# A retention and two mixture-of-experts layers on one core: the retention's state products in quarters of the array

## The chip, the cores and the metric

The kernel runs on one core of a Trainium2 chip. The metric is the device time of one execution in microseconds; of the kernel before, three runs are known, with a median of 594.36 us (592.88 to 595.75).

## What is computed

A retention (linear attention with a decay per head) over 4 batches, 8 heads, 768 tokens and 64 features feeds a soft mixture of experts, and that a top-2 mixture of experts. Only the first is touched by the change:

```python
gamma = 1.0 - 2.0 ** (-5.0 - np.arange(H, dtype=np.float32))
scale = 1.0 / np.sqrt(D)
state = np.zeros((B, H, D, D), dtype=np.float32)
for t in range(S):
    state = gamma[None, :, None, None] * state + np.einsum('bhd,bhe->bhde', k[:, :, t], v[:, :, t])
    y[:, :, t] = scale * np.einsum('bhd,bhde->bhe', q[:, :, t], state)
...
x = np.ascontiguousarray(attn_out.transpose(0, 2, 1, 3)).reshape(B * S, H * D)
x = _moe_ref(x=x, **moe_kwargs)
return _moe2_ref(x=x, **moe2_kwargs)
```

All of it is float32. The soft mixture needs the whole of x before its experts can start, so the retention (about the first 157 us) runs ahead of all else on TensorE; meanwhile SyncE's queue brings in q, k, v and the first expert weights (16 MB), and writes zeros to the output.

## The kernel before

The tokens are taken in 24 chunks of 128 (6 per batch, c = j % 6 is the place in the batch). A chunk's loop body (line 438) puts these steps on TensorE in this order; `put` ties each step behind the one before, so TensorE's order is the order of the text:

- `k_t(j+2)` (L281): four 128x128 transposes of K, copied out of PSUM by ScalarE (`kT`, L283).
- `inter(j)` (L310): the old state times Q, four products of 128x128 by 128x128. Two heads share a product: the state tile `sbd` is block-diagonal, so half of each is zeros. Not in the first chunk of a batch.
- `q_t` (L269): four transposes of Q, scaled out of PSUM by VectorE (`qT`, L274).
- `x_n(j-1)` (L343): four transposes of the last chunk's output `xT`, copied out by ScalarE (`x`, L345).
- `group1` (L381, `pd`), in every fourth chunk (j % 4 == 2).
- `qk(j+1)` (L292): eight products over 64 features, masked out of PSUM by VectorE into two `am` tiles (L296).
- `group0` (L354, `pl`) in chunks with j % 4 == 0 and `group2` (L391, `pp`) in those with j % 4 == 2: the soft mixture's logits, a running softmax on ScalarE and VectorE (`LT`, `al`, `dT`), and its weighted sum.
- `kv(j)` (L332): the new state, eight products into `pS`, copied by ScalarE into the two diagonal blocks of the other `sbd` tile (L337, two copies of 64x256). Not in the last chunk of a batch.
- `y_out(j)` (L320): eight products of V with `am`, added to the `py` bank that inter began; VectorE scales it into `xT` (L323).

After that, `spread(j+3)` (L253, L254) rearranges K of a later chunk on ScalarE (two copies of 64x512, into `comp` or `kl`) and V on GpSimd. Where ScalarE does this within its own order is the scheduler's choice. Three uses of PSUM share one tag, `pt`, with two buffers: k_t, q_t and x_n take it in turn, so x_n writes where k_t wrote and waits until ScalarE has copied kT away. `py` has two buffers of one bank, `pa` two, `pS` and `pg` one each: all eight banks are taken.

The loads of W1 (L479) are paced: each waits for a one-element VectorE copy of a chunk's `xT` (L478). K's and V's loads (L237) wait until ScalarE and GpSimd have emptied the buffer they go to.

Of the kernel before, what the change touches and what calls it, by code (L numbers as in the profile page):

```python
# [9 lines left out]
F32 = mybir.dt.float32  # L10
# [32 lines left out]
F1, F2, F3, F4 = 2, 0, 0, 26  # L43
FA, FT = 6, 3
RL = 1
XB = 6
FS, FU, FV = 10, 2, 2
TZ = 0, 4
BIG = 8192.0
# [5 lines left out]
def _const_table():  # L55
    j = np.arange(P)
    tok = 2 * (j % 64) + j // 64
    gam = 1.0 - 2.0 ** (-5.0 - np.arange(H, dtype=np.float64))
    cols = {}
    cols["mask"] = (tok[:, None] <= tok[None, :]).astype(np.float64)  # L60
    i = np.arange(64)
    gq = gam[None, :, None] ** (2 * i[None, None, :] + (j // 64)[:, None, None]) / np.sqrt(D)
# [42 lines left out]
def kernel(ctx: ExitStack, tc: tile.TileContext, q, k, v, phi, w1, w2,  # L105
# [103 lines left out]
    with ExitStack() as actx:  # L209
# [31 lines left out]
        def spread(j):  # L241
# [8 lines left out]
            gs = slice(64 * g, 64 * g + 64)  # L250
            for r in range(2):
                rs = slice(64 * r, 64 * r + 64)
                nc.scalar.copy(KL[j][rs], RAW[u][0][gs, :, r, :])  # L253
                pool_ins[0] = nc.gpsimd.tensor_tensor(VL[j][rs], RAW[u][1][gs, :, r, :],  # L254
                                        gv[gs, r, t, :, None].to_broadcast([64, H, D]), op=OP.mult)

        QT, KT, AM = {}, {}, {}
        sbd = []
        for i in range(2):
            s_t = io.tile([P, HP, P], F32, name=f"sbd{i}", bufs=1)  # L260
            nc.vector.memset(s_t, 0.0)
            sbd.append(s_t)

        def q_t(t, s):
            if s == 0:
                QT[t] = io.tile([P, HP, 2, P], F32, name="qT", bufs=2)
            pt = psA.tile([P, HP, P], F32, name="pt", tag="pt")
            for hp in range(HP):
                mm = nc.tensor.transpose(pt[:, hp, :], QL[t][:, 2 * hp + s, :, :], ident)  # L269
            o = QT[t].rearrange("p h g (r i) -> p h g r i", r=2)  # L270
            i = pt.rearrange("p h (g i) -> p h g i", g=2)
            for r in range(2):
                rs = slice(64 * r, 64 * r + 64)
                nc.vector.tensor_tensor(o[64 * s:64 * s + 64, :, :, r, :], i[rs],  # L274
                                        gq[rs, :, s, None, :].to_broadcast([64, HP, 2, 64]), op=OP.mult)
            return mm

        def k_t(j):
            pt = psA.tile([P, HP, P], F32, name="pt", tag="pt")
            for hp in range(HP):  # L280
                mm = nc.tensor.transpose(pt[:, hp, :], KL[j][:, 2 * hp:2 * hp + 2, :], ident)  # L281
# [4 lines left out]
        def qk(j):  # L286
            t, g = divmod(j, 2)
            pa = [psA.tile([P, HP, P], F32, name="pa", tag="pa") for _ in range(2)]
            for hp in range(HP):
                for s in range(2):  # L290
                    r = slice(64 * s, 64 * s + 64)
                    mm = nc.tensor.matmul(pa[s][:, hp, :], KT[j][r, hp, :], QT[t][r, hp, g, :],  # L292
                                          start=True, stop=True)
            for s in range(2):
                a = io.tile([P, HP, P], F32, name="am", bufs=3)
                nc.vector.tensor_tensor(a, pa[s], mask_b, op=OP.mult)  # L296
                AM[j, s] = a
            return mm

        pS = psA.tile([P, HP, D], F32, name="pS", bufs=1)  # L300
# [4 lines left out]
        def inter(j):  # L305
            t, g = divmod(j, 2)
            c = j % NC
            PY[j] = psA.tile([P, HP, P], F32, name="py")
            for hp in range(HP if c else 0):
                mm = nc.tensor.matmul(PY[j][:, hp, :], sbd[c % 2][:, hp, :], QT[t][:, hp, g, :],  # L310
                                      start=(hp == 0), stop=False, skip_group_check=True)
            return mm if c else None

        def y_out(j):
            c = j % NC
            py = PY.pop(j)
            am = [AM.pop((j, s)) for s in range(2)]
            for hp in range(HP):
                for s in range(2):
                    mm = nc.tensor.matmul(py[64 * s:64 * s + 64, hp, :], VL[j][:, 2 * hp + s, :],  # L320
                                          am[s][:, hp, :], start=(not c and hp == 0), stop=True, skip_group_check=True)
            XT[j] = work.tile([P, HP, P], F32, name="xT", bufs=4)
            nc.vector.tensor_tensor(XT[j], py, gy[:, c, :, None].to_broadcast([P, HP, P]), op=OP.mult)  # L323
            return mm

        def kv(j):
            c = j % NC
            if c == NC - 1:
                return
            for hp in range(HP):  # L330
                for s in range(2):
                    mm = nc.tensor.matmul(pS[64 * s:64 * s + 64, hp, :], KL[j][:, 2 * hp + s, :],  # L332
                                     VL[j][:, 2 * hp + s, :], start=(c == 0 and hp == 0),
                                     stop=True, skip_group_check=True)
            for s in range(2):
                r = slice(64 * s, 64 * s + 64)
# [81 lines left out]
        fill(psA, "py", FS)  # L418
        load_q(0)
        nc.sync.dma_start(cta, csta)  # L420
        load_kv(0)
# [3 lines left out]
        spread(0)  # L425
        for s in range(2):
            put(q_t, 0, s)
        fill(psA, "py", FU)
        put(k_t, 0)
        fill(psA, "py", FV)  # L430
        load_q(2)
        spread(1)
        load_kv(2)
# [4 lines left out]
        for j in range(NCH + 1):  # L438
            t, g = divmod(j, 2)
            if j < NCH:  # L440

                if j + 2 < NCH:
                    put(k_t, j + 2)
                put(inter, j)
                tn, s = (t + 1, 1) if g == 0 else (t + 2, 0)
                if tn < NT:
                    put(q_t, tn, s)
# [55 lines left out]
        pm = psA.tile([P, 4], F32, name="pm", tag="py")  # L503
        nc.tensor.matmul(pm, psel, m4, start=True, stop=True)
        group1(mg)
        fill(psA, "pa", 3)
# [7 lines left out]
        pz = psA.tile([P, 1], F32, name="pz", tag="py")  # L514
# [11 lines left out]
        for kd in range(KD):  # L526
# [4 lines left out]
        ph = psA.tile([P, QF], F32, name="ph", tag="py")  # L531
# [570 lines left out]
```

## Time and profile before

| what | value |
|---|---|
| median of 3 runs | 594.36 us (592.88 to 595.75) |
| profiled execution | span 596.2 us (the page gives no other time of it) |
| TensorE busy | 551.9 us (93%) |
| VectorE, ScalarE, GpSimd busy | 43%, 41%, 38% |
| mean granted clock of TensorE | 0.96 of full speed |
| DMA, whole span | 111.76 MB, mean 187 GB/s |
| the 20 `inter` steps | 160 instructions, 22.5 us busy |
| the 24 `qk` steps | 384 instructions, 29.0 us busy |

A float32 product appears as two TensorE instructions with two weight loads, so a step of four products counts x8. Busy time is the union of the instructions' spans, and overlapping instructions count once. How long a step holds TensorE is therefore read from the start of its first instruction to the start of the next step's. An engine can be busy nearly all the time and still start a step only because another engine has just finished.

### The profile page before, as it was taken

The numbers are of one execution on the slowest core, as the hardware profiler recorded it, in microseconds if no ns is written. First come the engines' busy times: TensorE is split into PE (matmuls) and PEld (weight loads), VectorE is DVE, ScalarE is ACT, GpSimd is POOL, SyncE is SP. The second block draws the span as 40 slices with busy tenths as digits, with TensorE's granted clock in tenths as the row PEclk, the third lists the DMA queues.
The fourth block names the chain that finished last, engine by engine and source line by source line (L and its number), as shares of the span: only waits on it lengthen the run. The fifth ranks groups of instructions, "written<-read, shape, count | busy, mean of one in ns | idle before, by whom it ended". The sixth has DMA issues, their size and how long they took to land. (4 is left out here: it accounts for less than half of the span.)

```text
span 596.2 us, 10652 instructions
## 1 busy us (share of the span) xinstructions
PE 551.9 (93%) x4176; PEld 418.9 (70%) x4176; DVE 254.6 (43%) x521; ACT 242.4 (41%) x529; POOL 224.0 (38%) x214
## 2 busy tenths in 40 slices
PE   6899999699899888799999999999999999999990
PEld 3787878578553345677787787787787787787870
DVE  3467777375303177834425225235235234324200
ACT  3565746344202235325426246256345345334200
POOL 3434634141103055445344434435344345432331
PEclk9799999799899898989999999999999999999996
DMA  9999999996699962446567566566656653644232
GB/s 251 246 273 308 236 323 379 349 349 236 257 384 410 379 211 68 96 96 167 131 138 186 109 146 181 109 149 181 128 141 174 133 122 55 138 101 51 38 40 33
DMA packets 79453, 111.76 MB, mean 187 GB/s; under 512 B 10034, under 2 KB 51570, under 8 KB 78498
## 3 DMA queue, kind: packets, MB, share of 16 engines
q1 hardware_dynamic: 65488, 94.75, 49.3%
q0 software_dynamic: 9696, 14.37, 17.4%
q10 hardware_dynamic: 4210, 1.87, 1.1%
q8 instruction: 35, 0.57, 0.4%
q14 instruction: 24, 0.20, 0.1%
HBM read 87.92 MB, written 20.41 MB: 182 GB/s over the span
## 5 line engine op out<-in xcount | busy, mean ns | idle before, releaser
L924 PE MATMUL pyc<-wh,hhl 128*128 128x512 f32 x384 | 154.1, 401 | 0.2 <-issue 0.2
L926 PE MATMUL pyc<-wh,hhl 128*128 128x512 f32 x384 | 152.4, 397 | 0.0
L925 PE MATMUL pyc<-wl,hhl 128*128 128x512 f32 x384 | 150.8, 393 | 0.0
L905 POOL DMA_INDIRECT out_dram<-yo,lsa x49 | 77.2, 1576 | 159.7 <-DMA out_dram<-yo,lsa 35.9
L896 DVE SCALAR_TENSOR_TENSOR hhl<-phc,hhl 128x512 fp32r<-128x512 f32 (+1 forms) x128 | 66.8, 551 | 73.9 <-ACT hhl L894 68.6
L926 PEld LDWEIGHTS pyc<-wh,hhl 128*128 128x128 f32 x384 | 72.4, 189 | 16.9
L925 PEld LDWEIGHTS pyc<-wl,hhl 128*128 128x128 f32 x384 | 72.6, 189 | 15.3
L924 PEld LDWEIGHTS pyc<-wh,hhl 128*128 128x128 f32 x384 | 72.3, 188 | 15.2 <-issue 0.8
L933 ACT ACTIVATE yo<-pyc,cg 128x512 f32<-128x512 f32 x48 | 33.0, 688 | 117.5 <-PE pyc L926 108.7
L872 DVE TENSOR_TENSOR wl<-w,wh 128x1024 fp32r<-128x1024 f32 x32 | 39.1, 1225 | 56.3 <-ACT wh L866 56.3
L894 ACT ACTIVATE hhl<-phc 128x512 fp32r<-128x512 f32 (+1 forms) x128 | 58.9, 515 | 10.2 <-PE phc L891 9.0
L838 POOL DMA_INDIRECT cg<-ctab,lsa x49 | 51.9, 1059 | 19.7 <-issue 13.5
L866 ACT CAST wh<-w 128x1024 fp32r<-128x1024 f32 x32 | 33.5, 1049 | 35.6 <-DMA w<-in_moe_w_dram 27.7
L296 DVE TENSOR_TENSOR am<-pa,cta 128x512 f32<-128x512 f32 x48 | 33.1, 692 | 31.3 <-PE py L320 15.9
L254 POOL TENSOR_TENSOR comp<-raws,cta 64x512 f32<-64x512 f32 x24 | 24.9, 1038 | 46.9 <-PE py L320 29.0
L274 DVE TENSOR_TENSOR qT<-pt,cta 64x512 f32<-64x512 f32 x48 | 33.0, 688 | 21.4 <-PE pt L269 21.0
L891 PE MATMUL phc<-cts,gs 128*128 128x256 f32 (+1 forms) x192 | 36.6, 300 | 3.0 <-DVE hhl L896 1.8
L254 POOL TENSOR_TENSOR vl<-raws,cta 64x512 f32<-64x512 f32 x24 | 24.9, 1038 | 34.7 <-PE py L320 22.4
L891 PEld LDWEIGHTS phc<-cts,gs 128*128 128x128 f32 x192 | 29.4, 191 | 10.3 <-issue 3.4
L292 PE MATMUL pa<-qT,kT 64*128 64x128 f32 x384 | 29.0, 292 | 1.2 <-ACT kT L283 1.2
L292 PEld LDWEIGHTS pa<-qT,kT 64*128 64x128 f32 x384 | 24.3, 194 | 5.6 <-issue 4.0
L310 PE MATMUL py<-qT,sbd 128*128 128x128 f32 x160 | 22.5, 285 | 4.9 <-ACT sbd L337 4.9
(191 smaller groups left out, 684.1 us busy)
## 6 DMA issues: line engine op xcount, KB each, us to landing
w<-in_moe_w_dram SPq DMA_DIRECT2D x77, 512.0 KB
w<-in_moe_w_dram SPq DMA_DIRECT2D x11, 2048.0 KB
comp<-in_q_dram SPq DMA_DIRECT2D x12, 512.0 KB
raws<-in_k_dram SPq DMA_DIRECT2D x12, 512.0 KB
raws<-in_v_dram SPq DMA_DIRECT2D x12, 512.0 KB
out_dram<-w SPq DMA_DIRECT2D x6, 1024.0 KB
gs<-gr SPq DMA_DIRECT2D x112, 32.0 KB
w<-in_moe_w_dram SPq DMA_DIRECT2D x2, 1024.0 KB
```

The lines of the kernel that those rows point to most:

```text
L254: pool_ins[0] = nc.gpsimd.tensor_tensor(VL[j][rs], RAW[u][1][gs, :, r, :], gv[gs, r, t, :, None].to_broadcast([64, H, D]), op=OP.mult)
L292: mm = nc.tensor.matmul(pa[s][:, hp, :], KT[j][r, hp, :], QT[t][r, hp, g, :], start=True, stop=True)
L838: nc.gpsimd.indirect_dma_start(out=cg[:rows(b), i, :], out_offset=None, in_=ctab, in_offset=index(e, b, rows(b)))
L866: ins = nc.scalar.copy(wh, V2[e][:, 1024 * i:1024 * i + 1024])
L872: nc.vector.tensor_tensor(wl, V2[e][:, 1024 * i:1024 * i + 1024], WH[e][i], op=OP.subtract)
L891: nc.tensor.matmul(ph[:, w * i:w * i + w], GS[e][:, kf + i], CT[e, g][:, :w], start=True, stop=True)
L894: relu.append(nc.scalar.activation(h[:, :, :w], pv, AF.Relu))
L896: last = nc.vector.scalar_tensor_tensor(h[:, :, w + t0:w + t0 + 2 * P], pv[:, :, :2 * P], 0.0, h[:, :, :2 * P], op0=OP.max, op1=OP.subtract)
L905: nc.gpsimd.indirect_dma_start(out=out, out_offset=index(e, b, n), in_=y, in_offset=None, bounds_check=N - 1, oob_is_err=False, compute_op ...
L924: nc.tensor.matmul(py, hhl[:, kf, ts], wh, start=(kf == 0), stop=False)
L925: nc.tensor.matmul(py, hhl[:, kf, ts], wl, start=False, stop=False)
L926: nc.tensor.matmul(py, hhl[:, kf, tl], wh, start=False, stop=(kf == KF - 1))
```

## The change

The eight heads are paired as k and k+4 (index a = 0 or 1) instead of 2hp and 2hp+1, so that both halves of the contraction side hold a real 64x64 state. `sbd` becomes a plain 128x256 tile, filled by one copy, and needs no zeros. `inter` issues eight 64x64 products instead of four 128x128; product (kb, a) sits in row half a and column half kb % 2 of the array, and writes bank a of `py`, which now has two banks and one buffer. `y_out` takes the heads in natural order, four of `am` tile 0 and then four of tile 1. K is permuted when it is spread, so that its transposes bring heads k and k+4 together.

`inter(j)` moves from behind k_t(j+2) to behind qk(j+1); group1 and group2 move from j % 4 == 2 to j % 4 == 1, the chunk right after group0; the x tiles go from 6 buffers to 5, the qT tiles from 2 to 3.

```diff
-                nc.scalar.copy(KL[j][rs], RAW[u][0][gs, :, r, :])
+                nc.scalar.copy(KL[j][rs].rearrange("p (k a) d -> p a k d", a=2),
+                               RAW[u][0][gs, :, r, :].rearrange("p (a k) d -> p a k d", a=2))
...
-            PY[j] = psA.tile([P, HP, P], F32, name="py")
-            for hp in range(HP if c else 0):
-                mm = nc.tensor.matmul(PY[j][:, hp, :], sbd[c % 2][:, hp, :], QT[t][:, hp, g, :],
-                                      start=(hp == 0), stop=False, skip_group_check=True)
+            PY[j] = psA.tile([P, 2, HP, P], F32, name="py", tag="py", bufs=1)
+            for kb in range(HP if c else 0):
+                cs = slice(64 * (kb % 2), 64 * (kb % 2) + 64)
+                for a in range(2):
+                    r = slice(64 * a, 64 * a + 64)
+                    mm = nc.tensor.matmul(PY[j][cs, a, kb // 2, :], sbd[c % 2][r, kb, :], QT[t][r, kb, g, :],
+                                          start=(kb < 2), stop=False, skip_group_check=True)
...
-            for hp in range(HP):
-                for s in range(2):
-                    mm = nc.tensor.matmul(py[64 * s:64 * s + 64, hp, :], VL[j][:, 2 * hp + s, :],
-                                          am[s][:, hp, :], start=(not c and hp == 0), stop=True, skip_group_check=True)
+            for h in range(H):
+                a, kb = divmod(h, HP)
+                mm = nc.tensor.matmul(py[64 * (h % 2):64 * (h % 2) + 64, a, kb // 2, :], VL[j][:, h, :],
+                                      AM[j, a][:, kb, :], start=(not c and kb < 2), stop=True, skip_group_check=True)
...
-            for s in range(2):
-                r = slice(64 * s, 64 * s + 64)
-                nc.scalar.copy(sbd[(c + 1) % 2][r, :, r], pS[r])
+            nc.scalar.copy(sbd[(c + 1) % 2], pS)
...
-                put(inter, j)
...
-            if j % 4 == 2 and j > 4:
+            if j % 4 == 1 and j > 4:
                 put(group1, j // 4 - 1)
             if j < NCH:
 
                 if j + 1 < NCH:
                     put(qk, j + 1)
+                put(inter, j)
 
                 if j % 4 == 0 and j:
                     put(group0, j // 4 - 1)
-                if j % 4 == 2 and j > 4:
+                if j % 4 == 1 and j > 4:
                     put(group2, j // 4 - 1)
```

Three places show how the order moves. First TensorE in an ordinary chunk (j = 2), before (pt is written by k_t, q_t and x_n in turn, pa by qk, pS by kv, and py by inter and y_out):

```order
L281 MATMUL pt<-ct,comp 128x128 x4
L310 MATMUL py<-qT,sbd_105 128x128 x4
L269 MATMUL pt<-ct,comp 128x128 x4
L343 MATMUL pt<-ct,xT 128x128 x4
L292 MATMUL pa<-qT,kT 128x128 x8
L332 MATMUL pS<-vl,kl 64x64 x8
L320 MATMUL py<-am,vl 64x128 x8
```

and now:

```order
L282 MATMUL pt<-ct,comp 128x128 x4
L270 MATMUL pt<-ct,comp 128x128 x4
L346 MATMUL pt<-ct,xT 128x128 x4
L293 MATMUL pa<-qT,kT 128x128 x8
L314 MATMUL py<-qT,sbd_105 64x128 x8
L338 MATMUL pS<-vl,kl 64x64 x8
L323 MATMUL py<-am,vl 64x128 x8
```

The products with the state stood between two uses of pt and now stand between qk and kv, so k_t, q_t and x_n follow one another directly.

Second, ScalarE at chunks 15 and 16, before (the comp copies wait for a DMA, that of K for chunks 20 and 21):

```order
L345 COPY x<-pt 128x512 [waits PE_49]
L253 COPY comp<-raws 64x512 [waits DMAHW1_49,Activation_49]
L253 COPY comp<-raws 64x512 [waits Activation_49]
L337 COPY sbd_105<-pS 64x4x64 [waits PE_49]
L337 COPY sbd_105<-pS 64x4x64
L253 COPY kl<-raws 64x512 x2
L283 COPY kT<-pt 128x512 [waits PE_49,Activation_49]
```

and now:

```order
L348 COPY x<-pt 128x512 [waits PE_49]
L255 COPY comp<-raws 64x2x4x64 [waits DMAHW1_49,Activation_49]
L255 COPY comp<-raws 64x2x4x64 [waits Activation_49]
L340 COPY sbd_105<-pS 128x256 [waits PE_49]
L255 COPY kl<-raws 64x2x4x64 x2
L284 COPY kT<-pt 128x512 [waits PE_49,Activation_49]
```

One state copy is left of two; the copies of K still stand ahead of the state's and of kT's.

Third, ScalarE in the chunk after a group0 (j = 13), before (al and dT belong to the running softmax):

```order
L337 COPY sbd_107<-pS 64x4x64 [waits PE_49,Activation_49]
L337 COPY sbd_107<-pS 64x4x64 [waits Activation_49]
L367 ACTIVATE al<-al 128x1 [waits DVE_49]
L372 ACTIVATE dT,MZ<-LT,nm 128x128 [waits DVE_49,Activation_49]
L253 COPY comp<-raws 64x512 [waits DMAHW1_49]
L283 COPY kT<-pt 128x512 [waits PE_49]
L253 COPY comp<-raws 64x512
```

and now:

```order
L340 COPY sbd_106<-pS 128x256 [waits PE_49,Activation_49]
L255 COPY comp<-raws 64x2x4x64 [waits DMAHW1_49]
L370 ACTIVATE al<-al 128x1 [waits DVE_49]
L375 ACTIVATE dT,MZ<-LT,nm 128x128 [waits DVE_49,Activation_49]
L255 COPY comp<-raws 64x2x4x64
L284 COPY kT<-pt 128x512 [waits PE_49]
```

Both copies of K now stand ahead of kT's copy, where one stood behind it.

## Rows read from the trace of the kernel before

**Rows 1.** Stretches of the span: us, busy time (count) per engine, PEclk, DMA share, GB/s.

```profile
27.07:59.56 32.49, 31.76 (x427) 26.50 (x426) 22.31 (x42) 19.02 (x38) 12.46 (x12) 1.00 0.91 278
59.56:104.33 44.77, 43.84 (x605) 36.48 (x603) 32.30 (x64) 26.19 (x56) 20.88 (x21) 1.00 1.03 312
...
117.34:153.32 35.98, 35.17 (x473) 28.56 (x470) 22.62 (x45) 16.48 (x39) 8.31 (x8) 1.00 0.84 297
```

**Rows 2.** Timeline, kv of chunk 1 to kv of chunk 2: start, duration, engine, line.

```profile
27.07 0.69 PE L332 MATMUL pS<-comp 128*64 128x64 f32 x16
...
27.59 1.05 PE L320 MATMUL py<-am,comp 128*64 128x128 f32 x16
27.80 0.74 ACT L337 COPY sbd<-pS 64x256 f32<-64x256 f32 x2 [1.13 <-PE pS L332]
28.56 0.66 PE L281 MATMUL pt<-ct,comp 128*128 128x128 f32 x4
28.57 1.26 ACT L253 COPY comp<-raws 64x512 f32<-64x512 f32 x2
28.66 0.69 DVE L296 TENSOR_TENSOR am<-pa,cta 128x512 f32<-128x512 f32 x1 [0.80 <-PE py L320]
...
29.05 1.06 PE L310 MATMUL py<-qT,sbd 128*128 128x128 f32 x8
29.27 0.68 DVE L323 TENSOR_TENSOR xT<-py,cta 128x512 f32<-128x512 f32 x1
29.85 0.59 ACT L283 COPY kT<-pt 128x512 f32<-128x512 f32 x1
...
29.95 0.60 PE L269 MATMUL pt<-ct,comp 128*128 128x128 f32 x4
...
30.49 0.66 PE L343 MATMUL pt<-ct,xT 128*128 128x128 f32 x4
...
31.08 1.16 PE L292 MATMUL pa<-qT,kT 64*128 64x128 f32 x16
...
32.17 0.69 PE L332 MATMUL pS<-vl,kl 128*64 128x64 f32 x16
```

**Rows 3.** Waits of TensorE's weight loads, 20 to 157 us: total us, times, longest.

```profile
PEld pt L343 <- ACT kT L283: 5.9, 18, 0.7
```

**Rows 4.** Timeline of ScalarE, then of TensorE: the wait for K in chunk 16.

```profile
109.32 1.24 ACT L253 COPY comp<-raws 64x512 f32<-64x512 f32 x2 [5.39 <-DMA raws<-in_k_dram]
...
111.37 2.08 PE L310 MATMUL py<-qT,sbd 128*128 128x128 f32 x8 [4.90 <-ACT sbd L337]
...
116.33 1.08 PE L354 MATMUL pl<-xT,phis 128*32 128x128 f32 x32
117.34 0.69 PE L332 MATMUL pS<-comp 128*64 128x64 f32 x16
```

**Rows 5.** Stretches of TensorE after the wait for K: us, PE busy, PEclk, DMA share, GB/s.

```profile
111.40:115.40 4.00, 4.00 (x18) 0.50 1.04 414
```

**Rows 6.** Timeline of SyncE's queue: the issue of that K load.

```profile
97.33 4.76 SPq L237 DMA_DIRECT2D raws<-in_k_dram  x1
```

**Rows 7.** Timeline of ScalarE after a group0 (chunk 13).

```profile
89.35 0.20 ACT L367 ACTIVATE al<-al 128x1 f32<-128x1 f32 x1
...
89.84 0.60 ACT L253 COPY comp<-raws 64x512 f32<-64x512 f32 x1
90.47 0.59 ACT L283 COPY kT<-pt 128x512 f32<-128x512 f32 x1
91.08 0.62 ACT L253 COPY comp<-raws 64x512 f32<-64x512 f32 x1
```

**Rows 8.** Timeline of TensorE with group1 and group2 (chunk 14).

```profile
96.88 0.27 PE L381 MATMUL pd<-ct,dT 128*128 128x128 f32 x1
97.08 1.16 PE L292 MATMUL pa<-qT,kT 64*128 64x128 f32 x16
98.17 1.06 PE L391 MATMUL pp<-x,dn 128*32 128x512 f32 x8
```

More of the change, by code (lines that the diff above doesn't have):

```diff
@@ L45 @@
 RL = 1
-XB = 6
+XB = 5
+AB = 3
 FS, FU, FV = 10, 2, 2
@@ L259, with q_t @@
         for i in range(2):
[L260 to L266, printed above, removed]
+            sbd.append(io.tile([P, HP, D], F32, name=f"sbd{i}", bufs=1))
+        def q_t(t, a):
+            if a == 0:
+                QT[t] = io.tile([P, HP, 2, P], F32, name="qT", bufs=3)
             pt = psA.tile([P, HP, P], F32, name="pt", tag="pt")
-            for hp in range(HP):
-                mm = nc.tensor.transpose(pt[:, hp, :], QL[t][:, 2 * hp + s, :, :], ident)
-            o = QT[t].rearrange("p h g (r i) -> p h g r i", r=2)
-            i = pt.rearrange("p h (g i) -> p h g i", g=2)
+            for kb in range(HP):
+                mm = nc.tensor.transpose(pt[:, kb, :], QL[t][:, kb + HP * a, :, :], ident)
+            o = QT[t].rearrange("p k g (r i) -> p k g r i", r=2)
+            i = pt.rearrange("p k (g i) -> p k g i", g=2)
             for r in range(2):
                 rs = slice(64 * r, 64 * r + 64)
-                nc.vector.tensor_tensor(o[64 * s:64 * s + 64, :, :, r, :], i[rs],
-                                        gq[rs, :, s, None, :].to_broadcast([64, HP, 2, 64]), op=OP.mult)
+                nc.vector.tensor_tensor(o[64 * a:64 * a + 64, :, :, r, :], i[rs],
+                                        gq[rs, :, a, None, :].to_broadcast([64, HP, 2, 64]), op=OP.mult)
             return mm
@@ L279, in k_t @@
             pt = psA.tile([P, HP, P], F32, name="pt", tag="pt")
-            for hp in range(HP):
-                mm = nc.tensor.transpose(pt[:, hp, :], KL[j][:, 2 * hp:2 * hp + 2, :], ident)
+            for kb in range(HP):
+                mm = nc.tensor.transpose(pt[:, kb, :], KL[j][:, 2 * kb:2 * kb + 2, :], ident)
             KT[j] = io.tile([P, HP, P], F32, name="kT", bufs=2)
@@ L288, in qk @@
             pa = [psA.tile([P, HP, P], F32, name="pa", tag="pa") for _ in range(2)]
-            for hp in range(HP):
-                for s in range(2):
-                    r = slice(64 * s, 64 * s + 64)
-                    mm = nc.tensor.matmul(pa[s][:, hp, :], KT[j][r, hp, :], QT[t][r, hp, g, :],
+            for kb in range(HP):
+                for a in range(2):
+                    r = slice(64 * a, 64 * a + 64)
+                    mm = nc.tensor.matmul(pa[a][:, kb, :], KT[j][r, kb, :], QT[t][r, kb, g, :],
                                           start=True, stop=True)
-            for s in range(2):
-                a = io.tile([P, HP, P], F32, name="am", bufs=3)
-                nc.vector.tensor_tensor(a, pa[s], mask_b, op=OP.mult)
-                AM[j, s] = a
+            for a in range(2):
+                am = io.tile([P, HP, P], F32, name="am", bufs=AB)
+                nc.vector.tensor_tensor(am, pa[a], mask_b, op=OP.mult)
+                AM[j, a] = am
             return mm
@@ L307, in inter @@
             c = j % NC
-            PY[j] = psA.tile([P, HP, P], F32, name="py")
-            for hp in range(HP if c else 0):
-                mm = nc.tensor.matmul(PY[j][:, hp, :], sbd[c % 2][:, hp, :], QT[t][:, hp, g, :],
-                                      start=(hp == 0), stop=False, skip_group_check=True)
+            PY[j] = psA.tile([P, 2, HP, P], F32, name="py", tag="py", bufs=1)
+            for kb in range(HP if c else 0):
+                cs = slice(64 * (kb % 2), 64 * (kb % 2) + 64)
+                for a in range(2):
+                    r = slice(64 * a, 64 * a + 64)
+                    mm = nc.tensor.matmul(PY[j][cs, a, kb // 2, :], sbd[c % 2][r, kb, :], QT[t][r, kb, g, :],
+                                          start=(kb < 2), stop=False, skip_group_check=True)
             return mm if c else None
@@ L316, in y_out @@
             py = PY.pop(j)
-            am = [AM.pop((j, s)) for s in range(2)]
-            for hp in range(HP):
-                for s in range(2):
-                    mm = nc.tensor.matmul(py[64 * s:64 * s + 64, hp, :], VL[j][:, 2 * hp + s, :],
-                                          am[s][:, hp, :], start=(not c and hp == 0), stop=True, skip_group_check=True)
+            for h in range(H):
+                a, kb = divmod(h, HP)
+                mm = nc.tensor.matmul(py[64 * (h % 2):64 * (h % 2) + 64, a, kb // 2, :], VL[j][:, h, :],
+                                      AM[j, a][:, kb, :], start=(not c and kb < 2), stop=True, skip_group_check=True)
             XT[j] = work.tile([P, HP, P], F32, name="xT", bufs=4)
-            nc.vector.tensor_tensor(XT[j], py, gy[:, c, :, None].to_broadcast([P, HP, P]), op=OP.mult)
+            nc.vector.tensor_tensor(XT[j].rearrange("p (a h) t -> p a h t", a=2), py[:, :, :2, :],
+                                    gy[:, c, :].rearrange("p (a h) -> p a h", a=2)[:, :, :, None]
+                                    .to_broadcast([P, 2, 2, P]), op=OP.mult)
             return mm
@@ L329, in kv @@
                 return
[L330 to L336, printed above, removed]
-                nc.scalar.copy(sbd[(c + 1) % 2][r, :, r], pS[r])
+            for kb in range(HP):
+                for a in range(2):
+                    h = kb + HP * a
+                    mm = nc.tensor.matmul(pS[64 * a:64 * a + 64, kb, :], KL[j][:, 2 * kb + a, :], VL[j][:, h, :],
+                                          start=(c == 0 and kb == 0), stop=True, skip_group_check=True)
+            nc.scalar.copy(sbd[(c + 1) % 2], pS)
             return mm
@@ L417 @@
         ov = out.rearrange("(p a) d -> p a d", p=P)
-        fill(psA, "py", FS)
+        fill(psA, "py", FS, 1)
         load_q(0)
@@ L427 @@
             put(q_t, 0, s)
-        fill(psA, "py", FU)
+        fill(psA, "py", FU, 1)
         put(k_t, 0)
-        fill(psA, "py", FV)
+        fill(psA, "py", FV, 1)
         load_q(2)
@@ L443 @@
                     put(k_t, j + 2)
-                put(inter, j)
-                tn, s = (t + 1, 1) if g == 0 else (t + 2, 0)
+                tn, r = (t + 1, 1) if g == 0 else (t + 2, 0)
                 if tn < NT:
-                    put(q_t, tn, s)
+                    put(q_t, tn, r)
                 if g == 0 and t + 3 < NT:
@@ L502 @@
         nc.vector.tensor_scalar_mul(m4, col("bmask"), NM.pop())
-        pm = psA.tile([P, 4], F32, name="pm", tag="py")
+        pm = psA.tile([P, 4], F32, name="pm", tag="py", bufs=1)
         nc.tensor.matmul(pm, psel, m4, start=True, stop=True)
@@ L513 @@
         group2(mg)
-        pz = psA.tile([P, 1], F32, name="pz", tag="py")
+        pz = psA.tile([P, 1], F32, name="pz", tag="py", bufs=1)
         nc.tensor.matmul(pz, psel, zb, start=True, stop=True)
@@ L530 @@
                               psi.rearrange("p k (e s) -> p k e s", s=SL))
-        ph = psA.tile([P, QF], F32, name="ph", tag="py")
+        ph = psA.tile([P, QF], F32, name="ph", tag="py", bufs=1)
         for e in range(E):
```

5 lines of the change are left out of this document (3 added, 2 removed).

## Prediction

> **What bounds the kernel now.** I read the busy times first, then the stretches, then one chunk of the timeline, then who waits for whom. In the stretches [rows 1] TensorE looks like the bound: 31.76 of 32.49 us busy between kv of chunk 1 and kv of chunk 7, at the full clock. The timeline of one chunk says more [rows 2]. From kv at 27.07 to the next at 32.17 are 5.10 us. On TensorE, kv takes 0.52 to the start of the next step, y_out 0.97, k_t 0.49, inter 0.90, q_t 0.54, so that x_n starts 3.42 after kv; then x_n 0.59 and qk 1.09. ScalarE in the same time: two state copies from 27.80, two K copies from 28.57, kT from 29.85 to 30.44. x_n starts at 30.49, 0.05 after kT ends. Its tile needs the PSUM buffer that kT empties, and the list of waits says the same: x_n's weight loads waited for kT 18 times [rows 3]. So two paths of equal length end at x_n, TensorE's own and ScalarE's, and work taken off TensorE ahead of x_n is worth what ScalarE's path gives too, no more.
>
> A second bound stands in chunk 16. ScalarE waits 5.39 us for K of a later chunk, until 109.32, with the state copy queued behind it; TensorE stands 4.90 us [rows 4], and when it resumes it is granted half its clock for about 4 us [rows 5]. That K load was late because the DMA engines were full: their share is 1.03 from 59.56 to 104.33 [rows 1], and the queue needed 4.76 us to issue it [rows 6].
>
> **The quartered product.** No row shows products that split rows and columns at once. inter's 8 instructions hold TensorE 0.90, 0.112 each. It now has 16. If four ran at once it would be 4 x 0.112 = 0.45. qk's 16 run two at a time and take 1.09 where 8 x 0.112 = 0.90 would do [rows 2]; pl's 32 run four at a time and take 1.01 where 0.90 would do [rows 4]. So entering another shape costs 0.11 to 0.19, and I take 0.60 (0.56 to 0.64). The ends are 0.45, and 0.90 if only two run at once. The Trainium skill (TensorEngine Tiling (Array Packing), Theoretical Speedup) gives up to 2x for each halved dimension: twice the products at a quarter of the time, 0.45. By that page the sum below would be 12 x 0.15 = 1.8 us lower; qk and pl stay behind it, so I stay with the rows.
>
> **An ordinary chunk.** From kv: the state copy starts after 0.73 as before, is one copy of 0.37 instead of 0.74 (its columns stay 256), then 0.03, K's copies 1.28, kT 0.59, 0.05: x_n can start at 3.05. The K copies write strided, but so did the old state copy, at the same time per column, so I leave them at 1.28. TensorE would be there at 0.52 + 0.97 + 0.49 + 0.54 = 2.52. VectorE: y_out now frees the first am tile after its first four heads, so the second mask can start 0.49 earlier, at 1.10; 0.69 for it and 0.68 for xT give 2.49. ScalarE ends last, by 0.5. From x_n: 0.59, qk 1.09, inter 0.60, kv. The sum is 3.05 + 0.59 + 1.09 + 0.60 = 5.33 against 5.10: **0.23 longer**. inter leaves a place where ScalarE's path covered it and goes to one where nothing does; the saved state copy gives back 0.37 of its 0.60.
>
> **Chunks with group1.** The 0.20 of pd and about 1.0 of pp [rows 8] move one chunk earlier and cost the same there. But ScalarE's order right behind group0 has both K copies and the softmax pair ahead of kT: 0.37 + 1.22 + 0.49 + 0.59 where it was 0.74 + 0.49 + 0.60 + 0.59 [rows 7], and inter comes on top. I take +0.5 in chunks 9, 13 and 17. Chunks 6, 12 and 18 have no inter: 0. In 21 to 23 no K copies are left, x_n waits for xT at 2.5, and inter's saving of 0.3 goes into that wait: 0.
>
> **The rest.** One y buffer of two banks: inter(j+1) needs xT(j) done, and x_n, ahead of it, waits for that already: 0. The x tiles go down to 5 and group2 uses them one chunk sooner: 0. SyncE's and GpSimd's queues keep their order; GpSimd's 12.46 of 32.49 us [rows 1] leaves room. The zeros of the old state tiles fall away in front of the first loads, which cover them: 0. Behind the retention every load hangs on TensorE's progress, so the rest shifts as a whole.
>
> **The sum.** To kv of chunk 7: five chunks with inter, 5 x 0.23 = +1.1. From there to chunk 15 the loss (seven such chunks, two of them after group0, about 2.2) falls into the wait for K and costs nothing. K itself lands later by what TensorE lost before the DMA filled up, 0 to 1.1; I take 0.7. After K lands, kv(16) came 8.02 later [rows 4]. Now x_n comes after K's copies 1.26, one state copy 0.37, K's next copies 1.28, kT 0.59 and 0.06 of gaps: 3.56; then 0.59 + 1.09 + 0.60 + 1.01 = 3.29, and 4 us at half clock as before add 2.0 [rows 5]: 8.85, so +0.8. Behind it, chunk 17 +0.5, chunks 19 and 20 +0.23 each: +1.0. Together 0.7 + 0.8 + 1.0 = **+2.5 us**. The profiled execution took 596.2, 1.8 above the median of the runs, and would take 598.7; the median becomes 594.36 + 2.5 = **596.9**. Bounds of my terms: inter at 0.45 or 0.90 in 12 chunks that count, -1.8 or +3.6; the half clock not granted at all or over the whole 3.29, -2.0 or +1.3; K's landing -0.7 or +0.4. The forecast's own range is 594 to 600.
>
> **Rivals.**
> - *TensorE paces, and the change gains.* If ScalarE's path is shorter than I read it (the copies overlap, or kT is not what ends last), x_n starts at 2.52 and a chunk takes 2.52 + 0.59 + 1.09 + 0.60 = 4.80, 0.30 less. With inter at 0.45 that is 0.45 less in five chunks before the DMA is full (-2.2) and in six behind the wait (-2.7), with +0.6 at the wait itself (0.8 less 0.15 for the cheaper inter): -4.3, **590.1**. For it: TensorE's 98% busy [rows 1]. Against: x_n 0.05 behind kT [rows 2], and the K copies stay ahead of kT in ScalarE's order.
> - *The quarters run two at a time.* The two row halves may block each other as the second of a pair, or each change of shape may cost more: inter 0.90, 12 x 0.30 = 3.6 more, +6.1, **600.5**. From 0.64 on, the loss is over 0.5%. For it: qk stays 0.19 above its ideal. Against: pl runs four at once and stays 0.11 above.
> - *The wait for K ends kindly.* TensorE stands shorter before x_n, its clock is not lowered, and K lands no later: 2.5 - 2.0 - 0.7 = -0.2, **594.2**. For it: TensorE reaches the wait about 2 us later than before. Against: it still idles some 4 us.
>
> **How the numbers follow.** Forecast 0.48, TensorE paces 0.22, two at a time 0.14, kind wait 0.16. About 0.5%, 3 us, is what a measurement of this kernel can tell from no change: faster is below 591.4, slower above 597.3. The forecast lies close to that edge: 0.28 of its chance within, 0.20 above. TensorE paces: 0.17 faster, 0.05 within. Two at a time: 0.14 slower. Kind wait: 0.02 faster, 0.14 within. So 0.19 faster, 0.47 the same, 0.34 slower. The range from 590 to 600.5 leaves out the better half of the first rival and the worse half of the second.
>
> **What would show it.** Right: in an ordinary chunk kv to kv takes 5.2 to 5.4 us, x_n starts within 0.1 of kT's end, TensorE idles some 0.5 us before x_n, and inter holds TensorE 0.55 to 0.65. The wait for K in chunk 16 stays, now in front of x_n, and the retention ends some 2 us later, with the rest of the program unchanged. Wrong: chunks of 4.8 us, x_n waiting for nothing; inter at 0.45 or 0.90; no wait for K; or a stretch behind the retention that changes by more than the shift.

## The result, and the profile after

The change made the kernel **slower by about 4 us**: 599.85 us in the median against 595.75 for before, 19 runs each, side by side; the ratio is 1.0067 (95% interval 1.0046 to 1.0089). The profiled execution took 597.68 us, its span is 595.9.

The ordinary chunk after, in the timeline from kv of chunk 1 to kv of chunk 2 (start, duration, engine, line, in brackets the idle time before it and what ended it); it answers to [rows 2]:

```profile
25.08 0.69 PE L338 MATMUL pS<-comp 128*64 128x64 f32 x16
25.59 1.05 PE L323 MATMUL py<-am,comp 128*64 128x128 f32 x16
25.81 0.37 ACT L340 COPY sbd<-pS 128x256 f32<-128x256 f32 x1 [1.73 <-PE pS L338]
26.19 1.26 ACT L255 COPY comp<-raws 64x512 f32<-64x512 f32 x2
26.57 0.66 PE L282 MATMUL pt<-ct,comp 128*128 128x128 f32 x4
27.06 0.60 PE L270 MATMUL pt<-ct,comp 128*128 128x128 f32 x4
27.47 0.59 ACT L284 COPY kT<-pt 128x512 f32<-128x512 f32 x1
28.11 0.66 PE L346 MATMUL pt<-ct,xT 128*128 128x128 f32 x4 [0.45 <-ACT kT L284]
28.70 1.16 PE L293 MATMUL pa<-qT,kT 64*128 64x128 f32 x16
29.79 0.67 PE L314 MATMUL py<-qT,sbd 64*64 64x128 f32 x16
30.39 0.69 PE L338 MATMUL pS<-vl,kl 128*64 128x64 f32 x16
```

x_n starts 3.03 us after kv, 0.05 after kT ends, and TensorE has stood 0.45. The quartered product holds TensorE from 29.79 to 30.39, 0.60. kv to kv is 5.31; it was 5.10 [rows 2].

The list of waits of TensorE's weight loads over the retention (total, times, longest) answers to [rows 3]; the total holds the long wait in chunk 16 too:

```profile
PEld pt L346 <- ACT kT L284: 21.5, 20, 7.2
```

The stretches kv(1) to kv(7), to kv(15), to kv(16), and from there to the last y_out; they answer to [rows 1]. The last row is the half-clock stretch behind the wait, as in [rows 5]:

```profile
25.08:58.09 33.01, 30.21 (x469) 24.14 (x465) 22.42 (x43) 16.91 (x33) 12.47 (x12) 1.00 0.91 283
58.09:104.67 46.58, 42.04 (x662) 33.19 (x658) 31.81 (x65) 23.48 (x49) 20.89 (x21) 1.00 1.01 301
104.67:119.41 14.74, 7.79 (x113) 6.28 (x109) 3.70 (x7) 3.90 (x7) 2.08 (x2) 0.77 0.96 322
119.41:156.53 37.12, 33.56 (x523) 25.68 (x520) 22.41 (x45) 14.71 (x34) 8.31 (x8) 1.00 0.82 280
...
114.20:118.30 4.10, 4.09 (x36) 3.23 (x36) 0.69 (x1) 0.58 (x1) 0.00 (x0) 0.50 1.02 399
```

TensorE is no longer busy all the time: 30.21 of 33.01 us, where it was 31.76 of 32.49 [rows 1]. The work left it and the time did not. Chunk 16 in the timeline (SyncE's issue of the load, ScalarE, TensorE), as in [rows 4, 6]:

```profile
97.43 5.38 SPq L239 DMA_DIRECT2D raws<-in_k_dram  x1
...
110.78 1.24 ACT L255 COPY comp<-raws 64x512 f32<-64x512 f32 x2 [7.11 <-DMA raws<-in_k_dram]
...
114.20 1.11 PE L346 MATMUL pt<-ct,xT 128*128 128x128 f32 x4 [6.95 <-ACT kT L284]
115.25 2.08 PE L293 MATMUL pa<-qT,kT 64*128 64x128 f32 x16
117.26 1.13 PE L314 MATMUL py<-qT,sbd 64*64 64x128 f32 x16
118.32 1.16 PE L357 MATMUL pl<-xT,phis 128*32 128x128 f32 x32
119.41 0.69 PE L338 MATMUL pS<-comp 128*64 128x64 f32 x16
```

The wait for K was not shortened by the loss ahead of it: it went from 5.39 to 7.11 us on ScalarE.

The table counts from kv(1) to x_n(23), the last step of the retention on TensorE, so that the start plays no part: kv(1) came at 27.07 before and at 25.08 after, and that the half-clock stretches in front of it, which lie in different places, make this difference was not tried. The second profile of the change, from the experiments, stands beside the first:

| stretch | before | after | after, again | predicted |
|---|---|---|---|---|
| kv(1) to kv(7) | 32.49 | +0.52 | +0.54 | +1.1 |
| kv(7) to kv(15) | 44.77 | +1.81 | +1.81 | +2.2 |
| kv(15) to kv(16) | 13.01 | +1.73 | +0.91 | -1.8 |
| kv(16) to x_n(23) | 39.10 | +0.90 | +0.91 | +1.0 |
| sum | 129.37 | +4.96 | +4.17 | +2.5 |

The prediction's -1.8 is its +1.5 at kv(16) (0.7 + 0.8) less the 1.1 and 2.2 that it had lost by then. The sums lie close to the 4.1 us between the medians. The two profiled executions as wholes do not show it: their spans are 596.2 and 595.9 us. Outside the retention one execution differs from another by as much: from the first product of the top-2 mixture's second layer (`pyc`) to the end it was 366.5 us before, 363.5 after and 365.1 after again, and the order of that part was not touched.

### The profile page after: what moved, and what is told of

It is laid out like the page before. It is cut to its first block, busy times and chain, and to the rows that moved or that the text cites. A ratio compares the mean times of both kernels' runs of the same rounds, so it can differ in the third digit from the quotient of the medians.

```text
span 595.9 us, 10956 instructions
## 1 busy us (share of the span) xinstructions
PE 543.9 (91%) x4336; PEld 406.6 (68%) x4336; DVE 253.3 (43%) x519; ACT 234.2 (39%) x509; POOL 223.3 (37%) x214
## 5 line engine op out<-in xcount | busy, mean ns | idle before, releaser
L841 POOL DMA_INDIRECT cg<-ctab,lsa x49 | 50.5, 1031 | 21.2 <-issue 15.5
L346 PE MATMUL pt<-ct,xT 128*128 128x128 f32 x96 | 16.1, 292 | 18.3 <-ACT kT L284 16.8
```

The lines of the kernel that those rows point to most:

```text
L841: nc.gpsimd.indirect_dma_start(out=cg[:rows(b), i, :], out_offset=None, in_=ctab, in_offset=index(e, b, rows(b)))
```

## The experiments

Theory: ScalarE's order (state, K, K^T) sets x_n's start, so inter, moved behind x_n, is paid in full; and the wait for K does not take up the loss, but has its own cause. Rivals: quarters that are cheap nowhere; a wait that is the change's own doing. The ratio of each version is against before, run beside it. "kv to kv" is kv(1) to kv(2), kv(15) to kv(16) is called the step to chunk 16, and "retention" is kv(1) to x_n(23), all from one profile of each version.

| version | kv to kv | kv(15) to kv(16) | retention | ratio (95% interval) |
|---|---|---|---|---|
| before | 5.10 | 13.01 | 129.37 | 1 |
| the change | 5.31 | 14.74 | 134.33 | 1.0067 (1.0046 to 1.0089) |
| the change, again | 5.32 | 13.92 | 133.54 | 1.0064 (1.0033 to 1.0095) |
| e1: x_n late | 4.79 | 15.13 | 123.43 | 0.9879 (0.9828 to 0.993) |
| e2: before, inter moved | 6.17 | 7.43 | 143.54 | 1.0191 (1.0124 to 1.0258) |
| e3: zeros later | 5.31 | 6.20 | 125.84 | 0.9935 (0.9897 to 0.9972) |
| e4: K^T first | 5.15 | 6.16 | 124.70 | 0.989 (0.9833 to 0.9947) |
| e5: x_n late, zeros later | 4.79 | 6.28 | 114.06 | 0.9713 (0.9626 to 0.98) |
| e5 again | 4.79 | 9.63 | 117.55 | 0.9764 (0.9715 to 0.9813) |
| e6: x_n late, K^T first | 4.79 | 5.80 | 121.03 | 0.9828 (0.9745 to 0.9912) |
| e7: before, order of e1 | 5.09 | 6.10 | 124.30 | 0.9922 (0.9883 to 0.996) |
| e8: before, zeros later | 5.10 | 7.86 | 124.31 | 0.9902 (0.9861 to 0.9943) |
| e9: e7, zeros later | 5.09 | 10.64 | 125.32 | 0.9891 (0.9847 to 0.9934) |
| e10: e5, zeros still later | 4.79 | 5.80 | 113.61 | 0.9789 (0.9752 to 0.9827) |

**x_n behind qk (e1).** The change, with group1 and qk ahead of x_n:

```diff
+            if j % 4 == 1 and j > 4:
+                put(group1, j // 4 - 1)
+            if j + 1 < NCH:
+                put(qk, j + 1)
             if j:
                 if j == NCH:
                     put(group0, NG - 1)
                 put(x_n, j - 1)
-            if j % 4 == 1 and j > 4:
-                put(group1, j // 4 - 1)
             if j < NCH:
-
-                if j + 1 < NCH:
-                    put(qk, j + 1)
                 put(inter, j)
```

> The changed kernel with x_n moved behind qk, so that kT's copy has 1.1 us more before its PSUM buffer is written again. Theory (x_n's wait for kT costs what the quarters save): TensorE no longer idles in an ordinary chunk, and kv to kv falls from 5.31 us to about 0.52 + 0.97 + 0.49 + 0.54 + 1.09 + 0.50 + 0.60 = 4.7. What is gained before the wait for K in chunk 16 is lost in that wait, which grows by some 4 us; behind it six chunks gain 0.6 each, so the whole is 3 to 5 us shorter than the changed kernel, about 595 to 597, ratio to the kernel before 0.998 to 1.002. Rival (the quartered products, or y's single buffer, are what costs): kv to kv stays at 5.2 to 5.3 with a wait in another place, the whole near 600, ratio 1.005 or more.

It took 592.15 us, a ratio of 0.9879 where 0.998 to 1.002 was expected. TensorE's timeline for one chunk, and the stretch kv(1) to kv(7):

```profile
32.59 0.66 PE L282 MATMUL pt<-ct,comp 128*128 128x128 f32 x4
33.08 0.60 PE L270 MATMUL pt<-ct,comp 128*128 128x128 f32 x4
33.61 1.16 PE L293 MATMUL pa<-qT,kT 64*128 64x128 f32 x16
34.70 0.66 PE L346 MATMUL pt<-ct,xT 128*128 128x128 f32 x4
35.29 0.67 PE L314 MATMUL py<-qT,sbd 64*64 64x128 f32 x16
35.89 0.69 PE L338 MATMUL pS<-vl,kl 128*64 128x64 f32 x16
...
26.31:56.10 29.79, 29.79 (x469) 24.13 (x465) 22.30 (x42) 16.91 (x34) 12.47 (x12) 1.00 0.96 293
```

No step waits, and TensorE is busy all of 29.79 us. qk's 1.09 us now cover ScalarE's path to x_n, and the chunk is the sum of TensorE's steps, 4.79. The step to chunk 16 grew to 15.13, so part of the gain went into the wait for K.

**inter moved, full width (e2).** Before, with nothing but inter's place changed (`put(inter, j)` from behind k_t to behind qk).

> The kernel before with one part of the change alone: inter goes behind qk, still as four full products with two state copies and two y buffers. Theory (the place of inter is what costs): x_n still starts 3.42 us after kv, since kT ends then, and inter's 0.90 comes on top behind qk: kv to kv 6.0 instead of 5.10. Six chunks before the DMA is full and seven behind the wait for K: ratio 1.010 to 1.018. Rival (the quarters or y's single buffer cost): nothing of them is in here, ratio 0.998 to 1.003.

It took 610.05 us, a ratio of 1.0191, a little over the 1.010 to 1.018 expected. TensorE's timeline, one chunk from kv at 25.50:

```profile
28.91 0.65 PE L343 MATMUL pt<-ct,xT 128*128 128x128 f32 x4 [0.82 <-ACT kT L283]
29.49 1.16 PE L292 MATMUL pa<-qT,kT 64*128 64x128 f32 x16
30.59 1.16 PE L310 MATMUL py<-qT,sbd 128*128 128x128 f32 x8
```

x_n stays 3.41 us behind kv, as before, though inter has left TensorE's path to it; TensorE now waits 0.82 there, and inter's 1.08 (0.90 expected, its cost before [rows 2]) comes on top. That is the theory's point: ahead of x_n, ScalarE's path is as long as TensorE's. Against the change (5.31) the chunk is 0.86 longer: 0.38 from the second state copy (x_n at 3.41 and 3.03), 0.48 from inter (1.08 and 0.60). One thing is mixed in: with two q^T buffers, VectorE's next q^T waits for inter in every second chunk (0.40 us); the chunks are alike all the same (6.17 and 6.24).

**Zeros later (e3, e8).** The change, and before, with the writes of zeros to the output two chunks later:

```diff
-Z0, ZN = 11, 6
+Z0, ZN = 13, 6
```

> The changed kernel with the six writes of zeros to the output two chunks later (j = 13 to 18 instead of 11 to 16), so that about 2 MB less stands in the queue ahead of the K load of chunks 20 and 21. Theory (the wait for K in chunk 16 swallows what TensorE loses or gains ahead of it, and costs a stretch at half clock): K lands 3 to 6 us sooner, TensorE's wait before x_n falls from 7 us to under 3, and the whole is 3 to 6 us shorter than the changed kernel. Rival (K is late because of W1's loads, or the later zeros delay what comes next): the wait stays at 5 us or more, or the weights of the soft mixture arrive late, and the whole is the same or longer.

> Before with the writes of zeros two chunks later, and nothing else. If the wait for K is independent of the change: the step to chunk 16 falls from 13.0 to 6.1 us, kv to kv stays 5.1 us, and the run is 5 to 7 us shorter (ratio 0.988 to 0.992), so that the change stands against it as it stood against before (some 4 us longer). If the wait depended on where TensorE was, as it swallowed 2 us of the change's early start: 2 to 4 us shorter.

594.99 and 592.77 us; by the ratios 7.9 us (0.0132 of 597) under the change, where 3 to 6 was expected, and 5.8 (0.0098) under before. The wait for K is there with and without the change, and goes in both, down to a rest of 2.46 us on ScalarE in before's, whose step is 7.86 instead of the 6.1 expected. SyncE's issue of the K load, ScalarE's copy of that K, now without a wait, and the step to chunk 16, in the change with zeros later:

```profile
97.76 0.38 SPq L239 DMA_DIRECT2D raws<-in_k_dram  x1
...
103.84 1.26 ACT L255 COPY comp<-raws 64x512 f32<-64x512 f32 x2
...
106.05:112.25 6.20, 5.87 (x112) 4.80 (x109) 3.70 (x7) 2.68 (x5) 2.08 (x2) 1.00 0.98 361
```

Issuing takes 0.38 us where it took 5.38, and the clock stays whole. Without the wait the change's retention is 1.5 us longer than before's (125.84 and 124.31), and would be some 3.2 longer if before's rest (7.86 - 6.20, the change's step) were gone too; some 4 had been expected.

**K^T first (e4).** The change, with K's spread copies held back on ScalarE until K^T of the chunk before has been copied:

```diff
+                with after(*([KTI[j - 1]] if j - 1 in KTI else [])):
+                    nc.scalar.copy(KL[j][rs].rearrange("p (k a) d -> p a k d", a=2),
+                                   RAW[u][0][gs, :, r, :].rearrange("p (a k) d -> p a k d", a=2))
...
-            nc.scalar.copy(KT[j], pt)
+            KTI[j] = nc.scalar.copy(KT[j], pt)
```

> The changed kernel with ScalarE's order turned: kT's copy ahead of the copies of K of a later chunk, in every chunk. Theory (ScalarE's copies ahead of kT set x_n): kT can start once k_t has ended, some 2.2 us after kv, and x_n starts at 2.85 instead of 3.03; kv to kv 5.1 in an ordinary chunk and 5.3 to 5.4 in the chunk after group0 without pp (5.6 now). The K copies no longer stand ahead of the state copy and of kT when K is late, so the wait in chunk 16 shrinks by some 3 us or moves to a later k_t: the whole 4 to 8 us shorter than the changed kernel. Rival (the K copies now come too late for k_t, or x's copy behind them holds TensorE): a new wait of 0.2 us or more in each chunk at k_t or q_t, and no gain.

594.51 us, a ratio 0.0177 under that of the change, some 10.6 us where 4 to 8 was expected. Timeline of TensorE and ScalarE in chunk 2, and of TensorE in chunk 19:

```profile
27.22 0.66 PE L283 MATMUL pt<-ct,comp 128*128 128x128 f32 x4
27.71 0.60 PE L271 MATMUL pt<-ct,comp 128*128 128x128 f32 x4
27.97 0.58 ACT L285 COPY kT<-pt 128x512 f32<-128x512 f32 x1 [1.14 <-PE pt L283]
28.58 1.25 ACT L256 COPY comp<-raws 64x512 f32<-64x512 f32 x2
28.61 0.66 PE L347 MATMUL pt<-ct,xT 128*128 128x128 f32 x4 [0.29 <-ACT kT L285]
...
124.07 0.63 PE L271 MATMUL pt<-ct,comp 128*128 128x128 f32 x4 [3.09 <-DMA comp<-in_q_dram]
```

ScalarE now waits for the transposes (1.14) and copies at once. x_n still waits 0.29: from k_t's start at 27.22 to the end of kT at 28.55 are 1.33 us, and only q_t stands between. So the chunk is 5.15 and not TensorE's 4.80; with x_n in that place, kT's copy alone sets it. The larger part of the gain is the step to chunk 16 (6.16): K's copy no longer stands in front of the state's and K^T's. A later wait takes part of it back: in chunk 19 q_t waits 3.09 us for its load of q.

**Both together (e6).** e1 and e4.

> The change with x_n behind qk and K^T's copy ahead of K's spread copies. TensorE is busy all the time with x_n late, so the earlier copy cannot shorten a chunk: 4.79 us again. But the spread copies can no longer stand one chunk ahead on ScalarE, in front of the state's copy and K^T's, when they wait for their load. If that place is what turns the late load of K into a stop of TensorE: the step to chunk 16 falls to some 6 us with 2 to 3 us of waiting left in a later chunk, and the run takes 584 to 589 us. If the load itself is what everything needs: 590 to 593, as with x_n moved alone.

587.32 us. 4.79 again, so the earlier copy gives nothing once qk covers it. The wait left chunk 16 (5.80) and stands in chunk 19, TensorE's timeline:

```profile
115.82 1.08 PE L271 MATMUL pt<-ct,comp 128*128 128x128 f32 x4 [4.56 <-DMA comp<-in_q_dram]
```

Several loads in a row are late, of q as well as K, and ScalarE's order decides which of them stops TensorE.

**x_n late, zeros later (e5, and again).**

> The change with x_n behind qk, and the writes of zeros two chunks later. If the long step to chunk 16 is the load of K competing with the writes of zeros, whatever the order of the work: kv to kv stays 4.79 us, the step to chunk 16 falls from 15.1 to some 5.8 us, the retention ends some 9 us earlier than with x_n moved alone, and the run takes 583 to 587 us (ratio to before 0.975 to 0.983). If what follows the retention has a bound of its own (its weights), the retention ends as early but the run stays at 589 to 593.

> The fastest version so far (quarters, x_n behind qk, zeros two chunks later) once more beside its full-width twin: 581 to 585 us, ratio to before 0.970 to 0.978, and 4 to 8 us under the twin.

583.07 and 585.29 us (the second 0.3 over the range given for it): the fastest version, ahead of both kernels. In the second profile ScalarE waited 4.1 us for K after all (step to chunk 16: 9.63), in the first 1.9 (6.28): the wait varies from one execution to the next.

**Quarters undone in the best order (e7, e9).** Before's full-width products in the order of e1, without and with zeros later; three q^T buffers, five of x, one state tile for room:

```diff
-            sbd.append(s_t)
+            sbd.extend([s_t, s_t])
...
-                QT[t] = io.tile([P, HP, 2, P], F32, name="qT", bufs=2)
+                QT[t] = io.tile([P, HP, 2, P], F32, name="qT", bufs=3)
```

> Before with its full-width products, in the order that was best with quarters: qk, x_n, inter, kv, the groups one chunk earlier, three q^T and five x buffers (one state buffer, for room; each product that reads it stands ahead of the product whose copy overwrites it). If the quarters are worth what they take off TensorE once nothing else paces it: TensorE is busy all the time, kv to kv is 4.79 + 1.06 - 0.60 = 5.25 us (4.79 + 0.56 = 5.35 at most), the retention ends 9 to 11 us later than with quarters in this order, and the run takes 599 to 604 us (ratio to before 1.003 to 1.013). If the order alone gave the gain and the quarters nothing: 4.8 to 5.0 us, 590 to 595 us.

> The full-width products in the order qk, x_n, inter, with the writes of zeros two chunks later: what the version with x_n late and zeros later is with quarters undone. In the traces of the two orders kv to kv was 5.09 us at full width and 4.79 with quarters. If that is all the quarters give, this one's retention ends 20 times 0.30 = 6 us later than with quarters and the run takes 587 to 591 us (ratio to before 0.980 to 0.988). If the order and the zeros are the whole gain: 582 to 585.

592.52 and 592.04 us. Both expectations missed: 599 to 604 for e7, 587 to 591 for e9. TensorE's timeline of e7, one chunk:

```profile
32.18 1.16 PE L292 MATMUL pa<-qT,kT 64*128 64x128 f32 x16
33.27 0.66 PE L343 MATMUL pt<-ct,xT 128*128 128x128 f32 x4
33.77 1.06 PE L310 MATMUL py<-qT,sbd 128*128 128x128 f32 x8
34.76 0.69 PE L332 MATMUL pS<-vl,kl 128*64 128x64 f32 x16
```

The chunk is 5.09, not 5.25 as I expected: inter takes 0.99 here and 0.60 in quarters, but x_n takes 0.50 ahead of a product of its own shape and 0.59 ahead of quarters (33.27 to 33.77; 34.70 to 35.29 in e1). So the quarters are worth 0.30 per chunk, some 6 us over 20 chunks, when nothing else paces TensorE; e9 and e5 again, timed side by side, lie 6.75 us apart. With the zeros in their old place the ratios of e7 and e1 lie only 0.0043 apart, some 2.6 us: e7 has no stand of TensorE in chunk 16, e1 the longest.

That is also why before's work in this order is faster than before (0.9922), though the chunk is 5.09 against 5.10: the step to chunk 16 fell from 13.01 to 6.10 with the zeros where they were. ScalarE's timeline in chunk 16, of e7 and then of e9:

```profile
102.70 0.59 ACT L283 COPY kT<-pt 128x512 f32<-128x512 f32 x1
105.44 1.24 ACT L253 COPY comp<-raws 64x512 f32<-64x512 f32 x2 [2.16 <-DMA raws<-in_k_dram]
...
105.02 1.25 ACT L253 COPY comp<-raws 64x512 f32<-64x512 f32 x2 [4.40 <-DMA raws<-in_k_dram]
106.78 0.76 ACT L337 COPY sbd<-pS 64x256 f32<-64x256 f32 x2
```

In e7 the copies that wait for K stand behind the state's copy and kT's of that chunk, and TensorE does not notice; in e9 the scheduler has put them ahead of both, as in before, and though K's copy comes 2.8 us sooner after kv(1) than in e7, the step takes 10.64. So the later zeros show no clear gain here (0.9922 and 0.9891, with overlapping intervals); by the traces it is because ScalarE's order changed along with them, though no run holds that order fixed. It fits e4: what a late load costs depends on what stands behind its copy.

**The change again.**

> The change itself once more, beside the versions that beat it, for a second profile of it. If the trace of the first was typical: the step to chunk 16 is 14 to 15 us, with ScalarE's copy of K waiting for its load, and the run is 2 to 5 us longer than before (ratio 1.003 to 1.009). If the longer wait for K was an accident of one run: the step is 13 us, and the run within 2 us of before.

601.04 us, against 597.44 for before. ScalarE's wait and SyncE's issue of that load:

```profile
98.06 5.60 SPq L239 DMA_DIRECT2D raws<-in_k_dram  x1
...
110.39 1.24 ACT L255 COPY comp<-raws 64x512 f32<-64x512 f32 x2 [5.73 <-DMA raws<-in_k_dram]
```

The first profile's 14.74 was at the long end, but the second too is longer than before's 13.01.

**Zeros still later (e10).** Z0 = 15. The last two of the six writes come after their source tile has been given to weights, so they write those in place of zeros; the traffic is the same, and only its time is read.

> The fastest version with the writes of zeros another two chunks later (chunks 15 to 20). In its second profile ScalarE still waited 4.1 us for K and the step to chunk 16 took 9.63 us instead of 5.80. If what is left of the wait is still the zeros' competition: the step is 5.8 us, no other chunk waits for its loads over 1 us, and the run takes 579 to 583 us (ratio to before 0.967 to 0.974). If the transfers are only pushed into the loads of the last chunks or of the stage behind the retention: a wait of 2 us or more there, and 583 to 588 us.

583.31 us. No wait for a load is left in the retention, the step is 5.80 as expected, and yet the run is no shorter than e5's. From x_n(23) to the first `pyc` product it took 77.6 us, where e5 took 75.8 and 74.9. That the pushed-back transfers do it would fit, but was not tried alone.

## Why the prediction was right and wrong

**Right: what paces a chunk.** 5.33 was forecast and 5.31 came, step by step: x_n at 3.05 (3.03), set by kT, then 0.59, 1.09 and 0.60. e2 shows that inter's old place was covered by ScalarE's path, and e1 that the chunk drops to 4.79 as soon as x_n does not stand there. The rival "TensorE paces" had that time, but not the way to it: e4 shows that even K^T's copy alone, without K's ahead of it, keeps x_n at 2.88. Two small readings on the way were off and cost nothing: VectorE's path adds up to 2.47, not 2.49, and 0.37 for 256 columns of the state beside 0.63 for 512 of K is not the same time per column; K's strided copies kept their 1.26 all the same.

**Right: inter at 0.60.** [rows 2, 4] gave it from the shapes beside it. The Trainium skill (TensorEngine Tiling (Array Packing), Theoretical Speedup) allows twice per halved dimension; between the same neighbours the traces have 0.99 and 0.60 (e7 and e1, x_n paying 0.09 besides) or 1.08 and 0.60 (e2 and the change), so the gain stays under that. The rival "two at a time" is out.

**Nearly right: the losses by chunk.** Chunks 2 and 3 lost 0.21 each, but 4 and 7 only 0.1, and 5 and 6 together gained 0.1: +0.52 for +1.1. Chunks 8 to 15 lost 1.81 for 2.2; of these, 9 and 10 together 0.53 and 13 and 14 together 0.90, where 0.73 (0.5 and 0.23) had been put down for each pair. Chunk 16 from K's landing (110.78) to kv took 8.63, and 9.18 in the second profile, for 8.85; TensorE worked at half clock for 4.3 us of it in the first and 5.5 in the second. Behind it, 0.90 for 1.0.

**Wrong: that the loss in chunks 8 to 15 "falls into the wait for K and costs nothing".** The step took K's arrival to be set by the full DMA engines, later by 0.7 only. It came later by 3.45 and 2.10 us. In times after kv(1), where "buffer free" is the end of the copy by which ScalarE empties the buffer that this load goes to:

| | kv(13) | buffer free | K's issue begins | K's copy starts | issue to copy |
|---|---|---|---|---|---|
| e1 | 61.76 | 64.14 | 67.30 | 79.30 | 12.00 |
| e7 | 65.11 | 67.92 | 69.22 | 80.86 | 11.64 |
| before | 65.89 | 68.65 | 70.26 | 82.25 | 11.99 |
| the change | 68.91 | 71.29 | 72.35 | 85.70 | 13.35 |
| the change, again | 68.93 | 71.31 | 72.02 | 84.35 | 12.33 |
| e2 | 77.15 | 79.89 | 80.23 | 89.91 | 9.68 |

Where TensorE is slower, the load is issued later, where faster, sooner; from issue to copy it is 11.6 to 13.4 us in all but e2. The copies that empty the buffer, in before and in the change:

```profile
94.46 1.26 ACT L253 COPY comp<-raws 64x512 f32<-64x512 f32 x2
...
95.11 1.26 ACT L255 COPY comp<-raws 64x512 f32<-64x512 f32 x2
```

The load cannot be issued ahead of them, as the description of the kernel says of K's and V's loads, and the prediction left it out. They end 2.64 us later after kv(1) in the change; the queue, still busy with issuing, reaches the load 1.61 us after that in before and 1.06 in the change. With zeros later it stands waiting, and e3's issue begins 0.02 us after the buffer is free (71.33 and 71.31). That is what [rows 1] could not show: full engines say that a transfer takes long, not that it starts at a fixed time. SyncE's queue waits for the work of earlier chunks at other loads too; of its list of waits from 60 to 105 us, in the change (L482 is a load of W1, L239 of K or V):

```profile
SPq L482 <- DVE w L481: 9.9, 5, 2.9
SPq L239 <- ACT kT L284: 5.1, 2, 5.0
SPq L239 <- ACT comp L255: 4.5, 1, 4.5
```

So the issue moves with the work, and the wait took up little or nothing of a loss of 2.33 us by kv(15). Of K's delay of 3.45 and 2.10, 2.09 and 1.76 stand in the issue; the other 1.36 and 0.34 passed between issue and copy, and why they differ is open. e2 bounds the statement: its loss by kv(15) was 13.4 us, issue to copy fell to 9.68, ScalarE waited 2.06 and the step took 7.43, so a large loss does shorten the wait. The -1.8 of the forecast became +1.73 and +0.91; the oversized losses took 1.1 back, and the sum was 5.0 and 4.2 instead of 2.5. The direction is as forecast, and each chunk's loss came the way that was forecast; but 2.33 of the 4.96 are losses ahead of the wait, of which the sum had kept only K's 0.7. The size, 0.67%, is beyond the 0.5% that the forecast lay close to, and 599.85 lies at the upper end of its 594 to 600: that the losses had been sized too large, by 1.1, is luck that hid part of the error. Of the 3.0 us between 596.9 and 599.85, 1.4 is the base: before was 594.36 in the three runs shown, and 595.75 in the 19 beside the change.

The rival "the wait ends kindly" went the other way: it became longer, and the clock was halved over 4.3 and 5.5 us of TensorE's work, where it was 4.1 before.

## To carry to other kernels

Before a cheaper instruction is put in, look at which engine's work ends last at the next joint: here TensorE's saving of 0.30 us a chunk turned into idle time until x_n was moved behind qk, and was then worth 6 us, or 2.6 where a wait for a load still came in between. Before a long wait for a transfer is counted on to swallow a loss ahead of it, find out whether the transfer's issue itself hangs on that work: read when its buffer comes free and what the queue waits for, not the DMA share. When a wait is due to competing transfers, move the competitor that nobody waits for; and look at what the waiting copy holds up behind it on its own engine, as e4 shows, and the steps of 6.10 and 10.64 us in e7 and e9.

## What was not expected of the hardware

A step on TensorE costs more beside a step of another tile shape. The full-width inter took 0.90 us between two steps of its own shape [rows 2], 0.99 with one such neighbour (e7) and 1.08 with none (e2); x_n took 0.50 ahead of its own shape and 0.59 ahead of another. It is not simply the step before or behind the change that pays: x_n behind qk took 0.50 in e7. The start-to-start cost of the eight 64x64 products, 0.60, may thus not be their own only.

The same program's wait for the same load differs between executions: 1.9 and 4.1 us on ScalarE in e5, 7.1 and 5.7 in the change. During a stand of 6.95 us in the change, and of 4.90 in before [rows 4], TensorE's granted clock fell to half (1.2 GHz), and stayed there for the first 4.3 and 4.1 us of the work that followed; in e3, where x_n waited 0.33 us in that chunk, it kept 2.4 GHz.

The way from x_n(23) to the first `pyc` product is not constant: 73.3 us before, 73.0 and 73.6 in the change, 71.5 to 73.3 in e2, e3, e6, e7, e8 and e9, but 74.9 to 77.6 in e1, e4, e5 and e10. Which transfers or half-clock stretches make the difference is open; for that reason the table has the retention beside the ratio.
